# Attention, MLP and mixture of experts in one kernel: early decay rows, fp32 partial sums, a fifth key block in 128 rows, expert conversions behind the slot numbers, eight slot tiles

## The chip, the cores and the metric

The kernel runs on one core of one Trainium2 chip. The metric is the device time of one execution in microseconds (us), the median of three runs. "The profiled execution" is one further run, taken with the hardware profiler; all rows below are from it.

## The reference

Three layers follow one another on 4 sequences of 576 tokens and 512 channels (8 heads of 64).

```python
def _attn_ref(q, k, v, f):                 # [4, 8, 576, 64], f: [4, 8, 576]
    scores = np.matmul(q, k.transpose(0, 1, 3, 2)) / sqrt(64)
    cum = np.cumsum(np.log(np.clip(f, 1e-4, 1)), axis=-1)
    scores = where(causal, -1e9, scores + cum[..., :, None] - cum[..., None, :])
    return softmax(scores) @ v
def _moe_ref(x, w_in, w_out):              # 2304 tokens, 512 -> 2048 -> 512
    h = np.maximum(x @ w_in, 0.0)
    return h * h @ w_out
def _moe2_ref(x, w_gate, w_noise, noise, w1, w2):   # 8 experts, 512 -> 1024 -> 512
    noisy = x @ w_gate + log1p(exp(x @ w_noise)) * noise
    # the two largest of 8 per token, softmax over these two,
    # out[token] += weight * (relu(x[token] @ w1[e]) @ w2[e])
```

## The kernel before, in words

Products are computed to nearly fp32 accuracy with fp16 operands: each operand is split into a high and a low half, and every product takes three matmuls (high x high, high x low, low x high). ScalarE (ACT) usually makes the high half, VectorE (DVE) the low one, and TensorE (PE) does the matmuls.

**Stages.** The first two query blocks of attention (the "head", in `hd_*`) run from a token list (`PLAN`) that fixes the order by hand, together with the first MLP pass. From then on the code is written step by step, and a scheduler orders each engine's instructions, held at places by `tc.issue_after(x)`: what is inside is issued on its engine after the instruction x.

**The MLP and its passes.** Tokens are taken in six chunks of 384 (`CH`); `mm1` makes the hidden block i of a chunk (12 matmuls, L585, then ReLU and squares on ACT, L592, L593, L596, and a difference on DVE, L601), and `mm2` adds it to the three output tiles `acc` in PSUM (9 matmuls, L647). The weights come as 64 bit words and are unpacked on arrival: three integer steps on DVE (L550, L555, L559), the high half on ACT (L562), the low half on DVE (L565). Since the weights arrive over time, chunks 0 and 1 run in two passes each: `passes` L1084 gives chunk 0 blocks 0 to 7, chunk 1 blocks 0 to 7, chunk 0 blocks 8 to 15, chunk 1 blocks 8 to 15, and then chunks 2 to 5 with all 16. Between, `spill` (L622) stores the half sum of a chunk to DRAM as a high and a low fp16 half (ACT L625, DVE L626), and `unspill` loads it; in `mm2` (L643 to 645) 12 matmuls with `ident2k`, a diagonal matrix of 2048, add it to the other half in PSUM. `x2_out` (L652) splits the sum into fp16 halves, stores it in `x2d` and transposes it.

**Attention beside it.** `att_tick` (L953) takes one unit (a batch, a query block i of 2 to 4, a pair of heads p) per tick, beside the MLP steps of passes three and on. `prep` (L189) prepares keys and queries of a pair in the tiles `setk` and `setq`; rows 64 to 69 hold the decay: those of `setk` come from DRAM by GpSimd's DMA queue (L202), those of `setq` are constants that GpSimd (POOL) fills once per pair in `make_set` (a memset L178 and two affine selects L179, L180). Query block 4 has 64 rows; both heads of a pair sit in the two halves of the array: L237 contracts 128 rows, L239 70 rows, the causal mask L243 64 rows. In `att_pv` (L305) the fifth key block, half filled, is multiplied in L323 with K = 64 rows, and key blocks 0 to 3 with 128.

**Router and experts.** After a chunk's MLP, `router` (L714) makes logits on PE (L724), then a long chain of small DVE and ACT operations; `slots` (L776) ranks tokens per expert with two matmuls and gives the slot numbers `si` (L792), with which GpSimd scatters the token numbers into `table` (L795). `slot_rows` (L856) loads a piece of `table` into a tile `tix` (six buffers, L860, on the SP queue), `gather` fetches these tokens (L871) and transposes them (L873, SP queue). `layer1` is L913 (relu and halves L917 on ACT, L918 on DVE), `layer2` L930, scaled by L933, and added to the output by an indirect DMA (L934). The expert weights come by `fetch_e` (L812, L816, five buffers `wr`, SP queue), and `split_e` converts them to halves (ACT L835, DVE L836); `split_next` (L846) converts one tile of 512 KB and issues the next load.

**Order of the last MLP chunk.** In chunk 5 the loop L1101 issues router and slots of chunk 4 at i = 2, five loads, from i = 4 on one `split_next` per step, then the table pieces and gathers of experts 0 and 1 at i = 6 and 9. After the chunk, `layer1(0, ...)`, `layer2(0, ...)`, expert 1, and then experts 2 to 7 follow.

Of the kernel before, what the change touches and what calls it, by code (L numbers as in the profile page):

```python
# [7 lines left out]
F32 = mybir.dt.float32  # L8
# [61 lines left out]
def attn_moe_moe_kernel(ctx: ExitStack, tc, qka, qk, v, fr, w_io, wgn, noise, w1, w2, out):  # L70
# [98 lines left out]
    ident2k = consts.tile([128, 128], F16, name="ident2k")  # L169
# [3 lines left out]
    def make_set(n):  # L173
        KK[n] = apool.tile([128, 2, 2, S], F16, name=f"setk{n}", tag=f"setk{n}", bufs=1)
        QQ[n] = apool.tile([128, 2, 2, REST], F16, name=f"setq{n}", tag=f"setq{n}", bufs=1)
        q2 = QQ[n][64:70, 1]
        with tc.issue_after(pin["pool"]):
            nc.gpsimd.memset(q2, -8.0)  # L178
            nc.gpsimd.affine_select(q2[:, 0], q2[:, 0], [[0, REST]], ALU.is_ge, 0.0, base=2, channel_multiplier=-1)  # L179
            nc.gpsimd.affine_select(q2[:, 1], q2[:, 1], [[0, REST]], ALU.is_ge, 0.0, base=-3, channel_multiplier=1)  # L180
# [35 lines left out]
    def att_s(u, pools):  # L216
# [12 lines left out]
        else:  # L229
            for hf in range(2):  # L230
# [74 lines left out]
    def att_pv(u):  # L305
# [325 lines left out]
    def unspill(c):  # L631
        for t in range(NT):
            if t % 2 == 0:
                bk = astream.tile([128, 2, 2 * DM], F16, name="bk", tag="pr", bufs=3)
            back[t] = bk[:, t % 2, :]
            nc.sync.dma_start(back[t], part[CH * c + 128 * t:CH * c + 128 * t + 128, :])
# [667 lines left out]
```

## Time and profile before

| what | value |
|---|---|
| median of three runs | 978.59 us (976.27 to 986.29) |
| profiled execution, its own time | 981.3 us |
| its span, first to last instruction | 979.1 us |
| mean granted TensorE clock | 0.983 |
| PE busy | 944.0 us (96%) |
| DVE, ACT, POOL busy | 570.3, 445.6, 209.4 us |

The time is read against the span: the profiled execution's own time has 2.2 us around its span. In the rows, L12 is line 12 of the kernel before; a busy time in brackets of a share is of the span; "idle before" is time in which the engine had nothing running just before the instruction, and the releaser is what ended it. PEclk is the granted TensorE clock as a share of full speed.

### The profile page before, as it was taken

How to read it: one execution, taken by the hardware profiler on the slowest of the kernel's cores; microseconds unless marked ns; L12 is line 12 of the kernel's file. 1: busy time of each engine (PE TensorE's matmuls, PEld its weight loads, DVE VectorE, ACT ScalarE, POOL GpSimd, SP SyncE). 2: the span in 40 equal slices, each digit the busy share in tenths (PEclk: the TensorE clock that was granted, in tenths of full speed). 3: DMA queues.
4: the chain of work that ended last, by engine and by line, in shares of the span. 5: the costliest groups of instructions: out<-in, count | busy, mean ns of one | idle time of the engine just before them, and what ended most of it. 6: DMA issues, size and time to landing. Idle time of an engine off the chain costs nothing.

```text
span 979.1 us, 17623 instructions
## 1 busy us (share of the span) xinstructions
PE 944.0 (96%) x6866; PEld 547.8 (56%) x6866; DVE 570.3 (58%) x1253; ACT 445.6 (46%) x990; POOL 209.4 (21%) x249
## 2 busy tenths in 40 slices
PE   6899989999999999999999899999999999999996
PEld 5766544554555555555555344657474756565662
DVE  6878888777787788776485241525252534334220
ACT  4775758767486566645473110414141323222110
POOL 2000141014041032011002316232232323111102
PEclk7999999999999999999999899999999999999998
DMA  7367858997979949746493914597958484941303
GB/s 301 118 242 224 200 149 267 176 215 172 224 156 250 204 89 234 144 55 99 106 332 113 210 37 97 106 219 174 241 144 188 129 194 96 236 82 27 42 12 43
DMA packets 219879, 155.34 MB, mean 159 GB/s; under 512 B 175698, under 2 KB 186322, under 8 KB 217746
## 3 DMA queue, kind: packets, MB, share of 16 engines
q1 hardware_dynamic: 207234, 124.75, 51.6%
q0 software_dynamic: 12416, 29.31, 14.3%
q8 instruction: 55, 0.90, 0.4%
q10 hardware_dynamic: 144, 0.13, 0.1%
q14 instruction: 30, 0.25, 0.1%
HBM read 89.05 MB, written 23.98 MB: 115 GB/s over the span
## 4 chain that ended last, share of the span: by engine, by line
PE 71%; DMA 8%; issue 7%; DVE 5%; POOL 3%; ACT 2%; SPq 2%; POOLq 0%; DVEq 0%; ACTq 0%
PE e L913 18%; PE e L930 17%; PE m L585 13%; PE acc L647 12%; PE po L320 2%; SPq L873 1%; DMA wr<-in_w_dram 1%; DMA w<-in_w_io_dram 1%; POOL table L795 1%; PE psab L398 1%; PE ps L226 1%; PE ps L227 1%; DMA pt<-phl 1%; PE po L323 1%; DMA xg<-x2d,tix 1%
## 5 line engine op out<-in xcount | busy, mean ns | idle before, releaser
L930 PE MATMUL e<-w2s,hT 128*128 128x512 f16 (+1 forms) x960 | 211.1, 382 | 2.0 <-ACT hT L917 1.3
L913 PE MATMUL e<-xgT,w1s 128*128 128x310 f16 (+2 forms) x1536 | 207.7, 297 | 4.1 <-DMA xgT<-xg 4.1
L647 PE MATMUL acc<-w,g 128*128 128x512 f16 x864 | 205.4, 380 | 0.0
L913 PEld LDWEIGHTS <-w1s 128*128 128x128 f16 x1536 | 140.3, 98 | 70.3 <-issue 8.2
L585 PE MATMUL m<-xT,w 128*128 128x384 f16 x960 | 173.7, 331 | 4.9 <-ACT r L592 3.7
L917 ACT ACTIVATE hT<-e 128x310 f16<-128x310 f32 (+2 forms) x128 | 54.7, 428 | 268.2 <-PE e L913 267.9
L930 PEld LDWEIGHTS <-hT 128*128 128x128 f16 (+1 forms) x960 | 99.8, 104 | 110.1 <-issue 2.2
L585 PEld LDWEIGHTS <-w 128*128 128x128 f16 x1152 | 109.9, 99 | 81.0 <-issue 10.4
L647 PEld LDWEIGHTS <-g 128*128 128x128 f16 x864 | 81.0, 98 | 86.2 <-DVE g L603 0.3
L933 DVE TENSOR_SCALAR y<-e,gs 128x512 f32<-128x512 f32 (+1 forms) x40 | 30.0, 750 | 159.3 <-PE e L930 133.8
L918 DVE SCALAR_TENSOR_TENSOR hT<-e,hT 128x310 f16<-128x310 f32 (+2 forms) x128 | 60.6, 477 | 80.7 <-ACT hT L917 80.4
L934 POOL DMA_INDIRECT out_dram<-y,tix x40 | 65.0, 1625 | 169.6 <-DVE y L933 125.1
L795 POOL DMA_INDIRECT table<-ent,si x36 | 41.4, 1149 | 166.0 <-DVE si L792 156.6
L592 ACT ACTIVATE r<-m 128x384 f32<-128x384 f32 x80 | 39.2, 490 | 68.1 <-PE m L585 67.7
L255 DVE TENSOR_REDUCE sm<-ps 128x1 f32<-128x384 f32 (+2 forms) x96 | 53.1, 562 | 22.1 <-PE ps L243 8.7
L871 POOL DMA_INDIRECT xg<-x2d,tix x40 | 44.3, 1108 | 83.6 <-DMA xgT<-xg 73.3
L258 ACT ACTIVATE pr<-ps,sm 128x384 f32<-128x384 f32 (+1 forms) x64 | 40.2, 630 | 25.8 <-DVE sm L257 23.4
L593 ACT ACTIVATE g<-r 128x384 f16<-128x384 f32 x96 | 50.1, 521 | 3.2 <-PE acc L647 1.5
L836 DVE SCALAR_TENSOR_TENSOR w2s<-wr,w2s 128x1024 f16<-128x1024 f32 x32 | 39.1, 1223 | 19.8 <-ACT w2s L835 19.8
L602 DVE TENSOR_TENSOR r<-r 128x384 f32<-128x384 f32 x64 | 35.4, 553 | 25.2 <-ACT g L593 24.9
L836 DVE SCALAR_TENSOR_TENSOR w1s<-wr,w1s 128x1024 f16<-128x1024 f32 x32 | 39.0, 1225 | 12.7 <-ACT w1s L835 12.5
L279 DVE TENSOR_TENSOR phl<-pr,phl 128x384 f16<-128x384 f32 (+1 forms) x64 | 38.5, 619 | 13.2 <-ACT phl L278 12.8
(281 smaller groups left out, 1085.2 us busy)
## 6 DMA issues: line engine op xcount, KB each, us to landing
wr<-in_w_dram SPq DMA_DIRECT2D x64, 512.0 KB, 5.2
qkr<-in_qk_dram SPq DMA_DIRECT2D x16, 896.0 KB, 6.0
w<-in_w_io_dram SPq DMA_DIRECT2D x8, 1024.0 KB, 4.8
w<-in_w_io_dram POOLq DMA_DIRECT2D x8, 1024.0 KB, 5.7
vr<-in_v_dram SPq DMA_DIRECT2D x16, 320.0 KB, 4.5
x2d<-x SPq DMA_DIRECT2D x18, 256.0 KB, 2.7
hraw<-in_qka_dram SPq DMA_DIRECT2D x8, 512.0 KB, 5.9
out_dram<-zero SPq DMA_DIRECT2D x5, 768.0 KB, 5.2
```

Source lines behind the costliest of these rows:

```text
L255: seen[u] = nc.vector.tensor_reduce(sm[:, z:z + 1], ps[z][:, :N], AX.X, ALU.max).ins
L585: nc.tensor.matmul(ps, W[i][:, wi, 0, 128 * cc:128 * cc + 128], xT[:, xi, cc, r0:r0 + CH], start=(x == 0), stop=(x == 11))
L593: nc.scalar.activation(g[:, 0, :], r, AF.Square, scale=2.0 ** -10)
L647: last[0] = nc.tensor.matmul(acc[t], g[:, gi, 128 * t:128 * t + 128], W[i][:, wi, 1, :], start=(i in ends[c][0] and x == 0), stop=(i in en ...
L795: s_ = nc.gpsimd.indirect_dma_start(out=table, out_offset=bass.IndirectOffsetOnAxis(ap=si[:, t, k:k + 1], axis=0), in_=ent[:, t, k, :], in ...
L836: nc.vector.scalar_tensor_tensor(lo, t_, sc, hi, op0=ALU.mult, op1=ALU.subtract)
L871: nc.gpsimd.indirect_dma_start(out=xg, out_offset=None, in_=x2d[0:seen, :], in_offset=bass.IndirectOffsetOnAxis(ap=rows_t[key, j][0], axis=0))
L913: last[0] = nc.tensor.matmul(ps[:, :hw], w1s[:, cc, wi, 128 * i:128 * i + 128], xgT[:, 4 * xi + cc, c], start=(x == 0), stop=(x == 11)).ins
L917: relu[0] = nc.scalar.activation(hi, ps[:, :hw], AF.Relu).ins
L918: nc.vector.scalar_tensor_tensor(hT[:, i, 1, c], ps[:, :hw], 0.0, hi, op0=ALU.max, op1=ALU.subtract)
L930: last[0] = nc.tensor.matmul(ps[:m], hT[:, i, hi, 128 * j:128 * j + m], w2s[:, i, wi, :], start=(i == 0 and x == 0), stop=(i == NFE - 1 an ...
L934: s_ = nc.gpsimd.indirect_dma_start(out=out, out_offset=bass.IndirectOffsetOnAxis(ap=ix[:m], axis=0), in_=y[:m], in_offset=None, compute_o ...
```

## The change

It has five parts.

1. `make_q` is taken out of `make_set`. The `setq` constants of pairs 0, 1 and 3 are filled in the token `consts` at the start; pair 2, whose storage first holds another tile (`identf`), stays where it was.
2. The half sums are stored as fp32: `spill` is one ACT copy, `unspill` loads all three tiles with one DMA, the 12 matmuls with `ident2k` go, and `x2_out` adds the half sum on DVE before it makes the halves.
3. In the fifth block, L323 uses all 128 rows for each key block, and the mask L243 all 128 rows.
4. In the last MLP chunk the five first weight loads wait for the store of chunk 4's last output tile; conversions are issued behind `si` of chunk 4 (eight of them in the chunk, for i from 4 to 11); the other eight (expert 1) are issued one per step of expert 0's first layer, each behind a ReLU of that layer.
5. `tix` and `gs` have eight buffers instead of six.

```diff
-    ident2k = consts.tile([128, 128], F16, name="ident2k")
     def make_set(n):
         KK[n] = apool.tile([128, 2, 2, S], F16, name=f"setk{n}", tag=f"setk{n}", bufs=1)
+        if n not in QQ:
+            with tc.issue_after(pin["pool"]):
+                make_q(n)
+
+    def make_q(n):
         QQ[n] = apool.tile([128, 2, 2, REST], F16, name=f"setq{n}", tag=f"setq{n}", bufs=1)
         q2 = QQ[n][64:70, 1]
-        with tc.issue_after(pin["pool"]):
-            nc.gpsimd.memset(q2, -8.0)
...
+        nc.gpsimd.memset(q2, -8.0)
...
-                        nc.tensor.matmul(ps[r, 224:288], identw[0:64, 0:64], maskw[0:64, 0:64], start=False, stop=True, skip_group_check=True)
+                        nc.tensor.matmul(ps[r, 224:288], identw[:, 0:64], maskw[:, 0:64], start=False, stop=True, skip_group_check=True)
...
-            K = 128 if kb < 4 else 64
...
-                nc.tensor.matmul(po[64 * h:64 * h + 64, p // 2, 0, p % 2, :], pt[:K, kb, pi, 64 * h:64 * h + 64],
-                                 vs[:K, kb, h, vi, :], start=first, stop=last, skip_group_check=True)
+                nc.tensor.matmul(po[64 * h:64 * h + 64, p // 2, 0, p % 2, :], pt[:, kb, pi, 64 * h:64 * h + 64],
+                                 vs[:, kb, h, vi, :], start=first, stop=last, skip_group_check=True)
...
-    part = dram.tile([2 * CH, 2 * DM], F16, name="part")
+    part = dram.tile([2 * CH, DM], F32, name="part")
...
-            nc.scalar.activation(sp[:, :DM], acc[t], AF.Copy, scale=2.0 ** -11)
-            nc.vector.scalar_tensor_tensor(sp[:, DM:], acc[t], 2.0 ** -11, sp[:, :DM], op0=ALU.mult, op1=ALU.subtract)
+            sp = gpool.tile([128, DM], F32, name="sp", tag="x2", bufs=3)
+            nc.scalar.activation(sp, acc[t], AF.Copy)
...
+        back[c] = astream.tile([128, NT, DM], F32, name="bk", tag="w64", bufs=2)
+        nc.sync.dma_start(back[c], part[CH * c:CH * c + CH, :].rearrange("(t p) d -> p t d", p=128))
...
-            if i == NA + 4 and c < 2:
-                for z in range(2):
-                    nc.tensor.matmul(acc[t], ident2k, back[t][:, DM * z:DM * z + DM], start=False, stop=False)
...
+            src = acc[t]
+            if c < 2:
+                src = back[c][:, t]
+                nc.vector.tensor_tensor(src, acc[t], src, op=ALU.add)
...
-        nc.vector.tensor_copy(si, sf)
+        slotted[0] = nc.vector.tensor_copy(si, sf).ins
...
-        tix = epool.tile([128, NJ, 2], I32, name="tix", bufs=6)
+        tix = epool.tile([128, NJ, 2], I32, name="tix", bufs=8)
-        gs = epool.tile([128, NJ], F32, name="gs", bufs=6)
+        gs = epool.tile([128, NJ], F32, name="gs", bufs=8)
...
+            for n in (0, 1, 3):
+                make_q(n)
...
         if (c, i) == (NCH - 1, 2):
-            for _ in range(WR):
-                fetch_next()
-        if c == NCH - 1 and i >= 4:
-            split_next()
+            with tc.issue_after(x2_put[0]):
+                for _ in range(WR):
+                    fetch_next()
+        if c == NCH - 1 and 4 <= i < 12:
+            split_next(slotted[0])
...
-    while at["split"] < 16:
-        split_next()
...
+    def begin(i):
+        split_next(relu[0])
+        if i == NR1:
+            lastp.append(router(NCH - 1, (psE, "e2", 2, 512), last[0]))
```

The order of instructions on four engines shows what moves. First ACT at the border of the second and third pass, before; `m` is the PSUM tile of `mm1` (one buffer), `w` a weight tile, `sp` a tile of the half sums of chunk 1, `acc` its accumulators:

```order
L592 ACTIVATE r<-m_1567 128x384
L562 ACTIVATE w_1499<-w_1267 128x1024
L593 ACTIVATE g<-r 128x384
L625 ACTIVATE sp<-acc_1182 128x512
L625 ACTIVATE sp<-acc_1186 128x512
L596 ACTIVATE r<-r 128x384
L625 ACTIVATE sp<-acc_1190 128x512
L592 ACTIVATE r<-m_1595 128x384
L562 ACTIVATE w_1561<-w_1433 128x1024
```

and of the change:

```order
L594 ACTIVATE r<-m_1571 128x384
L595 ACTIVATE g<-r 128x384
L598 ACTIVATE r<-r 128x384
L627 ACTIVATE sp<-acc_1186 128x512
L627 ACTIVATE sp<-acc_1190 128x512
L564 ACTIVATE w_1565<-w_1437 128x1024
L627 ACTIVATE sp<-acc_1194 128x512
L594 ACTIVATE r<-m_1599 128x384
```

Before, L562 of one weight tile stands between a ReLU and its square, and L593, all three spills and the next ReLU stand behind it; of the change, the weight tile's L564 stands between the second and the third spill (its line is L562 shifted by two), behind the squares.

Second, DVE in the last MLP chunk, late in the router's chain of chunk 4, before; `oh`, `ent`, `mprev` are the router's small tiles, `w1s` and `w2s` expert weights, L602 and L603 the MLP's own step:

```order
L750 CAST idf<-i_6788 128x6
L836 SCALAR_TENSOR_TENSOR w2s<-wr,w2s 128x2x512
L602 TENSOR_TENSOR r<-r 128x384
L757 TENSOR_SCALAR dd<-ed 128x3
L765 TENSOR_SCALAR oh<-iota_139,idf 128x8 x6
L836 SCALAR_TENSOR_TENSOR w2s<-wr,w2s 128x2x512
L603 SCALAR_TENSOR_TENSOR g<-r,g 128x384
L758 RECIPROCAL ent<-dd 128x3
L761 TENSOR_SCALAR ent<-pid 128x2
L836 SCALAR_TENSOR_TENSOR w2s<-wr,w2s 128x2x512
L761 TENSOR_SCALAR ent<-pid 128x2 x2
L602 TENSOR_TENSOR r<-r 128x384
```

and of the change, from the end of that chain on (`sf` and `si` are the slot numbers, L837 is the conversion, L604 and L605 the MLP's step):

```order
L786 TENSOR_TENSOR rk<-pr__6797,base_139 128x8 x3
L604 TENSOR_TENSOR r<-r 128x384
L791 TENSOR_TENSOR sl<-oh,rk 128x3x8 x2
L605 SCALAR_TENSOR_TENSOR g<-r,g 128x384
L792 TENSOR_REDUCE sf<-sl 128x6
L793 CAST si<-sf 128x6
L837 SCALAR_TENSOR_TENSOR w1s<-wr,w1s 128x1024 x4
L837 SCALAR_TENSOR_TENSOR w2s<-wr,w2s 128x2x512
L946 TENSOR_SCALAR offs<-pe__6921 128x2
L604 TENSOR_TENSOR r<-r 128x384
L837 SCALAR_TENSOR_TENSOR w2s<-wr,w2s 128x2x512
```

Before, conversions stand between the router's operations; of the change none does before `si`, and five stand in a row behind it.

Third, the queues of SP and POOL around the first layer of expert 2, here with the program's numbers. SP before (`tix_8782` and `tix_8786` are the table pieces of expert 4, the `wr` behind them weights of expert 3):

```order
L812 DMA wr_8309<-in_w1_dram 128x1024
L860 DMA tix_8782<-table_82 128x8
L816 DMA wr_8341<-in_w2_dram 128x2x512
L816 DMA wr_8402<-in_w2_dram 128x2x512
L860 DMA tix_8786<-table_82 128x2
L816 DMA wr_8436<-in_w2_dram 128x2x512
```

and of the change (`tix_9198` and `tix_9202` are the pieces of expert 5):

```order
L813 DMA wr_8286<-in_w1_dram 128x1024
L861 DMA tix_9198<-table_82 128x8
L817 DMA wr_8318<-in_w2_dram 128x2x512
L861 DMA tix_9202<-table_82 128x2
L817 DMA wr_8379<-in_w2_dram 128x2x512
L817 DMA wr_8413<-in_w2_dram 128x2x512
```

POOL at the last scatters of expert 1, before (`tix_7094` and `tix_7715` hold expert 1's rows; `xg_8791` to `xg_8800` are gathers for expert 4):

```order
L934 DMA out_0_dram<-y_8272,tix_7094 2944x512
L934 DMA out_0_dram<-y_8304,tix_7094 2944x512
L862 TENSOR_SCALAR gs_8784<-tix_8782 128x4
L871 DMA xg_8791<-x2d_81,tix_8782 128x1024
L871 DMA xg_8794<-x2d_81,tix_8782 128x1024
L871 DMA xg_8797<-x2d_81,tix_8782 128x1024
L871 DMA xg_8800<-x2d_81,tix_8782 128x1024
L934 DMA out_0_dram<-y_8336,tix_7715 2944x512
```

and of the change (`tix_7071` and `tix_7692` hold expert 1's rows):

```order
L935 DMA out_0_dram<-y_8249,tix_7071 2944x512
L935 DMA out_0_dram<-y_8281,tix_7071 2944x512
L863 TENSOR_SCALAR gs_9200<-tix_9198 128x4
L935 DMA out_0_dram<-y_8313,tix_7692 2944x512
L863 TENSOR_SCALAR gs_9204<-tix_9202 128x1
L872 DMA xg_8780<-x2d_81,tix_8763 128x1024
L872 DMA xg_9207<-x2d_81,tix_9198 128x1024
```

On SP, both table loads of expert 4 become loads of expert 5, and the second moves ahead of one more weight load. On POOL, the four gathers leave the place between the fourth and the fifth scatter of expert 1; the L863 in their place reads expert 5's piece of the table.

## Rows read from the trace of the kernel before

**Rows 1.** Page, part 1: busy us (share of the span) and instructions

```profile
PE 944.0 (96%) x6866; PEld 547.8 (56%) x6866; DVE 570.3 (58%) x1253; ACT 445.6 (46%) x990; POOL 209.4 (21%) x249
```

**Rows 2.** Waits of PE: waited for: us in total, times, longest

```profile
PE e L913 <- DMA xgT<-xg: 4.1, 1, 4.1
...
PE ps L227 <- DMA setk<-c: 1.4, 1, 1.4
```

**Rows 3.** Timeline of PE: start us, us, line, [idle before <-releaser]

```profile
138.93 2.12 PE L585 MATMUL m<-xT,w 128*128 128x384 f16 x12
144.31 3.69 PE L585 MATMUL m<-xT,w 128*128 128x384 f16 x12 [3.26 <-ACT r L592]
147.83 4.05 PE L647 MATMUL acc<-w,g 128*128 128x512 f16 x18
```

**Rows 4.** Timeline of PE around the start of expert 0

```profile
541.41 5.99 PE L647 MATMUL acc<-w,g 128*128 128x512 f16 x27
551.51 18.47 PE L913 MATMUL e<-xgT,w1s 128*128 128x512 f16 x72 [4.11 <-DMA xgT<-xg]
```

**Rows 5.** Timeline of PE, second layers of experts 1 and 2

```profile
683.01 4.69 PE L930 MATMUL e<-w2s,hT 128*128 128x512 f16 x21
...
690.35 22.73 PE L930 MATMUL e<-w2s,hT 128*128 128x512 f16 x97 [0.72 <-DVE hT L918]
...
738.30 26.06 PE L930 MATMUL e<-w2s,hT 128*128 128x512 f16 x120
```

**Rows 6.** Stretches: us, each engine's busy us, PEclk, DMA share, GB/s

```profile
139.00:149.00 10.00, 6.74 (x31) 3.39 (x30) 9.96 (x12) 7.29 (x12) 5.36 (x5) 0.83 0.30 98
551.00:558.00 7.00, 6.49 (x18) 2.41 (x19) 0.55 (x1) 0.60 (x1) 2.78 (x4) 0.56 0.98 225
689.00:695.00 6.00, 5.25 (x16) 1.90 (x17) 3.48 (x5) 1.34 (x2) 0.00 (x0) 0.72 1.08 321
```

**Rows 7.** Timeline of ACT at the border of passes two and three

```profile
140.46 1.14 ACT L562 ACTIVATE w<-w 128x1024 f16<-128x1024 f32 x1 [2.78 <-DVE w L559]
```

**Rows 8.** Groups by form, 133 to 145 us: busy us, mean ns

```profile
L179 POOL TENSOR_SCALAR_AFFINE_SELECT setq<-setq 6x320 f16<-6x320 f16 x4 | 5.0, 1262 | 0.1
...
L559 DVE SCALAR_TENSOR_TENSOR w<-w,w 128x1024 int32<-128x1024 int32 x2 | 2.9, 1466 | 0.0
```

**Rows 9.** Groups by form, the whole span

```profile
L871 POOL DMA_INDIRECT xg<-x2d,tix x40 | 44.3, 1108 | 83.6 <-DMA xgT<-xg 73.3 <-issue 10.3
...
L559 DVE SCALAR_TENSOR_TENSOR w<-w,w 128x1024 int32<-128x1024 int32 x16 | 20.0, 1249 | 0.1
...
L337 DVE TENSOR_TENSOR xs<-po,sums 128x512 f32<-128x512 f32 x16 | 11.0, 686 | 1.8 <-PE po L458 1.4 <-PE po L515 0.3
...
L626 DVE SCALAR_TENSOR_TENSOR sp<-acc,sp 128x512 f16<-128x512 f32 x6 | 3.9, 678 | 0.0
```

**Rows 10.** Chain that ended last, in order of time: start us, us, what

```profile
525.70 0.97 POOL table L795
...
547.18 4.19 DMA xgT<-xg
```

**Rows 11.** Groups by form of DVE, 495.8 to 525.4 us

```profile
L836 DVE SCALAR_TENSOR_TENSOR w2s<-wr,w2s 128x1024 f16<-128x1024 f32 x8 | 9.7, 1218 | 3.7 <-ACT w2s L835 3.7
```

**Rows 12.** Waits of the SP queue, the whole span

```profile
SPq L860 <- DMA out_dram<-y,tix: 94.3, 11, 15.1
```

**Rows 13.** Timeline of ACT in the second layer of expert 1

```profile
687.59 1.06 ACT L835 ACTIVATE w2s<-wr 128x1024 f16<-128x1024 f32 x1 [7.13 <-DMA wr<-in_w_dram]
```

**Rows 14.** Timeline of PE, one unit of a fifth block

```profile
220.67 0.32 PE L237 MATMUL ps<-setk,setq 128*64 128x288 f16 x2
220.79 0.32 PE L239 MATMUL ps<-setk,setq 70*64 70x288 f16 x2
221.04 0.28 PE L323 MATMUL po<-vs,pt 64*64 64x64 f16 x6
```

**Rows 15.** DMA issues: count, KB each, median us to landing

```profile
wr<-in_w_dram SPq DMA_DIRECT2D x64, 512.0 KB, 5.2
```

More of the change, by code (lines that the diff above doesn't have):

```diff
@@ L174, in make_set @@
         KK[n] = apool.tile([128, 2, 2, S], F16, name=f"setk{n}", tag=f"setk{n}", bufs=1)
+        if n not in QQ:
+            with tc.issue_after(pin["pool"]):
+                make_q(n)
+    def make_q(n):
         QQ[n] = apool.tile([128, 2, 2, REST], F16, name=f"setq{n}", tag=f"setq{n}", bufs=1)
         q2 = QQ[n][64:70, 1]
-        with tc.issue_after(pin["pool"]):
-            nc.gpsimd.memset(q2, -8.0)
-            nc.gpsimd.affine_select(q2[:, 0], q2[:, 0], [[0, REST]], ALU.is_ge, 0.0, base=2, channel_multiplier=-1)
-            nc.gpsimd.affine_select(q2[:, 1], q2[:, 1], [[0, REST]], ALU.is_ge, 0.0, base=-3, channel_multiplier=1)
+        nc.gpsimd.memset(q2, -8.0)
+        nc.gpsimd.affine_select(q2[:, 0], q2[:, 0], [[0, REST]], ALU.is_ge, 0.0, base=2, channel_multiplier=-1)
+        nc.gpsimd.affine_select(q2[:, 1], q2[:, 1], [[0, REST]], ALU.is_ge, 0.0, base=-3, channel_multiplier=1)
     xT = wpool.tile([128, 2, 4, RING], F16, name="xT")
@@ L631, in unspill @@
     def unspill(c):
[L632 to L636, printed above, removed]
+        back[c] = astream.tile([128, NT, DM], F32, name="bk", tag="w64", bufs=2)
+        nc.sync.dma_start(back[c], part[CH * c:CH * c + CH, :].rearrange("(t p) d -> p t d", p=128))
     def mm2(c, i):
@@ L650, in attn_moe_moe_kernel @@
     x2T_t = {}
+    x2_put = [None]
+    slotted = [None]
     def x2_out(c):
@@ L655, in x2_out @@
             x2T = gpool.tile([128, 8, 128], F16, name="x2T", bufs=3)
-            nc.scalar.activation(x2[:, :DM], acc[t], AF.Copy, scale=2.0 ** -10)
-            nc.vector.scalar_tensor_tensor(x2[:, DM:], acc[t], 2.0 ** -10, x2[:, :DM], op0=ALU.mult, op1=ALU.subtract)
+            src = acc[t]
+            if c < 2:
+                src = back[c][:, t]
+                nc.vector.tensor_tensor(src, acc[t], src, op=ALU.add)
+            nc.scalar.activation(x2[:, :DM], src, AF.Copy, scale=2.0 ** -10)
+            nc.vector.scalar_tensor_tensor(x2[:, DM:], src, 2.0 ** -10, x2[:, :DM], op0=ALU.mult, op1=ALU.subtract)
             r0 = SPARE + CH * c + 128 * t
             nc.sync.dma_start_transpose(out=x2T, in_=x2)
-            nc.sync.dma_start(x2d[r0:r0 + 128, :], x2)
+            x2_put[0] = nc.sync.dma_start(x2d[r0:r0 + 128, :], x2).ins
             x2T_t[t] = x2T
@@ L1024, in attn_moe_moe_kernel @@
             nc.gpsimd.memset(half[64:128], 1.0)
-            for t_, cmp, val in ((identw, ALU.not_equal, 1.0), (maskw, ALU.is_ge, -BIG), (ident2k, ALU.not_equal, 2048.0)):
+            for t_, cmp, val in ((identw, ALU.not_equal, 1.0), (maskw, ALU.is_ge, -BIG)):
                 nc.gpsimd.memset(t_, 0.0)
-                pin["pool"] = nc.gpsimd.affine_select(t_, t_, [[-1, 128]], cmp, val, base=0, channel_multiplier=1).ins
+                nc.gpsimd.affine_select(t_, t_, [[-1, 128]], cmp, val, base=0, channel_multiplier=1)
+            for n in (0, 1, 3):
+                make_q(n)
         elif tok[0] == "X" and tok[1] != "T":
@@ L1172, in attn_moe_moe_kernel @@
     ov = ctx.enter_context(tc.tile_pool(name="ov", bufs=1, side="left"))
-    while at["split"] < 16:
-        split_next()
     lastp = []
-    layer1(0, 0, NE0, lambda i: lastp.append(router(NCH - 1, (psE, "e2", 2, 512), last[0])) if i == NR1 else None, last[0])
+    def begin(i):
+        split_next(relu[0])
+        if i == NR1:
+            lastp.append(router(NCH - 1, (psE, "e2", 2, 512), last[0]))
+    layer1(0, 0, NE0, begin, last[0])
     layer2(0, 0, NE0, lambda j: slots(NCH - 1, lastp[0], (psE, "e2", 2, 512), last[0]) if j == 0 else None)
```

1 line of the change is left out of this document (removed).

## The prediction

> **What bounds the kernel now.** I read the page first. PE is busy for 944.0 of 979.1 us [rows 1], so the end is set by PE's work, its idle time and its clock; a gain elsewhere counts only where PE waits for it. The waits of PE come second: the longest with a fault that this change can touch are the one on `xgT` (4.1 us) and one on `setk` (1.4 us) [rows 2]. [...] Full rate is read from 120 matmuls of 512 columns in 26.06 us [rows 5]: 0.217 us each.
>
> The sums are made against the profiled execution's own time, 981.3 us, which is 2.7 above the median; I take the 2.7 off at the end.
>
> **Early decay rows.** At the border of the second and third pass, 12 matmuls end at 138.93 + 2.12 = 141.05, the next 12 wait 3.26 us for a ReLU and then take 3.69 instead of 2.12, and the 18 after them 4.05 instead of 18 x 0.217 = 3.9 [rows 3]. That is 3.26 + 1.57 + 0.15 = 5.0 us. The ReLU stands in ACT's order behind the spills and behind L562, which itself waited 2.78 us for the integer step L559 of a weight tile on DVE [rows 7]. DVE was late because POOL filled `setq` beside it: L559 took 1.466 us there and 1.249 over the whole span [rows 8, 9], a sixth more, while four fills of L179 alone held POOL for 5.0 us. Nine of the twelve fills leave this place, and ACT's order puts L562 behind the squares and two spills. I value this at 5.0, from 0 (something else holds the ReLU) to 5.4.
>
> The fills go to the start, where DVE is on the chain too. Nine fills, each at most the 1.262 us of L179 [rows 8], make 11.4 us of POOL; a sixth on DVE work all through it would be 2.0 us. DVE has gaps there (it waits for loads), and a late low half costs nothing until PE wants it, so I take the low side: 0.5, from 0 to 2.0. [...]
>
> **Order of setk.** PE's 1.4 us on `setk` [rows 2] come from GpSimd's DMA queue: the rows of one pair are issued behind six table scatters. Their order is now the other way for that pair: 1.4, from 0.
>
> **Half sums.** The 12 matmuls with `ident2k` stand in PE's stream without idle time around them: 12 x 0.217 = 2.6 us. In their place six DVE adds from PSUM come, nearest to L337 at 0.686 us; six L626 of 0.678 go [rows 9], so DVE has nothing more to do. The bytes in DRAM are the same. The adds lie behind the last matmul of a chunk, where the next chunk wants `acc` again one step later; each would have to hold it for a whole instruction to cost something. I take 2.6, from 1.5 to 2.6.
>
> **Fifth block in 128 rows.** Two L237 starts lie 0.12 us ahead of L239, but L239 with two such matmuls lies 0.25 ahead of L323 with 64 rows [rows 14]: a change of the row mode costs some 0.10 to 0.13. Of the modes in a unit (128 x 64, 64 x 64, back) two changes go, in each of 16 units, and again where the mask is: 32 to 36 changes of 0.10, so 3.4 us, from 1.7 (if the pipeline hides half) to 4.3. The wider matmuls have the same columns and cost nothing. [...]
>
> **Slot numbers first.** Expert 0 starts 551.51 - (541.41 + 5.99) = 4.1 us after the last MLP matmul, and its 72 matmuls take 18.47 instead of 72 x 0.217 = 15.6 [rows 4]: 7.0 us in all. What ended last is a chain: the scatters of the table begin at 525.70, right behind `si`, then table loads, gathers and their transposes until 551.4 [rows 10]. In the router's stretch before it DVE ran eight conversions of `w2s`, 9.7 us [rows 11], and four of `w1s` of the same size: 12 x 1.22 = 14.6 us among the router's small operations. None stands there now. If only 10 of the 14.6 come off, the chain ends at 541 and PE stops no longer: 7.0, from 0 to 7.0. What is late next is a conversion: eight stand behind `si` with MLP steps between them (1.22 us each against some 4 us of a step's PE work: 12 matmuls of 2.12 and 9 of 0.217 each), and eight in expert 0's first layer, one per step. I charge 1.5, from 0 to 4.
>
> **Eight slot tiles.** The second layer of expert 2 takes 690.35 + 22.73 - 683.01 = 30.1 us, that of expert 3 26.06 [rows 5]: 4.0 us lost. ACT waited 7.13 us there for a weight load [rows 13], because SP stood at a table load that needs a buffer whose last scatter had not landed; such waits reach 15.1 us [rows 12]. With eight buffers the table loads are not freed of this: they run one expert further ahead and still wait for expert 1's scatters, and three weight loads now stand behind the second instead of two. But the fifth scatter no longer stands behind four gathers on POOL, 4 x 1.108 = 4.4 us [rows 9] and their gaps. The weights then land about 5 us earlier, against the 4.0 that PE lost: just ahead of the need. I take 3.0 of the 4.0, from -1 to 4.0.
>
> **Sum.** 5.0 + 1.4 + 2.6 + 3.4 + 7.0 + 3.0 = 22.4 gained, 0.5 + 1.5 = 2.0 lost: 20.4. Own time 981.3 - 20.4 = 960.9, median about 958.2.
>
> **Rivals.**
> - *The border keeps its stop.* ACT, not DVE, may be what is full there: two conversions, three spills and four ReLU steps still pass. For it: L562 still stands ahead of the third spill. Against: DVE's fills explain the 2.78 us. Gain 15.4: 963.2.
> - *A new wait in the last chunk or at expert 0.* Five conversions stand together behind `si` while the MLP needs its low halves; a stop of about 3 us costs about 6 with the lower clock, as 4.1 cost 7.0 above. 964.2.
> - *Only the parts inside PE's stream work* (2.6 + 3.4 = 6.0), since the chain and the queues find other reasons to be late. 972.6. Against it: each stop has its own named cause.
> - *Slower: expert 0's first layer at the pace of its loads.* All eight conversions of expert 1 now sit in ACT's order among that layer's ReLUs, each behind a weight load on SP, and SP also has the transposes. A load lands in 5.2 us [rows 15], a step of PE takes 2.6. If loads don't run ahead and each step waits for its own, a step lasts 5.2 plus the conversion, about 7.4: 8 x 4.8 = 38 us, 958.2 + 38 = 996. It decides from the point where the five `wr` buffers are empty at the layer's start; against it, the loads for expert 1's first five tiles are issued in the last MLP chunk already.
>
> **Chances.** The forecast 0.65, the border 0.10, the new wait 0.12, only PE's stream 0.09, the slower one 0.04. About 1% (9.8 us) is what a measurement of this kernel tells from no change; faster than 968.8 are the first three: 0.87; within it the fourth: 0.09; slower 0.04. The range: with all terms at their good ends and no costs the gain is 23.8, and the other short waits of PE beside attention can move by 2 us either way, an estimate from the 1.4 of the one on `setk`: 952 down to a little less, 951; upward it takes in the border and the new wait and some of both: 968.
>
> **What would show it.** Right: no row of L645; PE without a stop between 139 and 148; no wait on `xgT` before expert 0; the block of expert 2 near 26 us; no wait on `setk`; granted clock near 1 in the three stretches. Wrong: a long wait of L585 on ACT near 140, a wait of expert 0's ReLU or second layer on `wr`, a longer start up to the first flips, or fifth blocks with unchanged spacing, which would take the 3.4 away.

## The result, and the profile after

The changed kernel takes 968.83 us (median of six runs, 964.07 to 971.47), the kernel before 978.92 beside it: a ratio of 0.9895, 95% interval 0.9864 to 0.9925. Forecast was 958, in a range of 951 to 968, so it is faster, but by half of what was forecast. Measured twice more, the ratio was 0.9828 (0.9792 to 0.9863) and 0.9859 (0.9823 to 0.9894), that is 17.0 and 12.2 us. Taken together, the gain is some 13 us, not 20.4. The three differ by more than their intervals say (the first and the second don't overlap), so a few us between two measurements prove little here. All ratios are of fast runs alone, which leaves one run of u4 (977.01 us) out of its ratio.

The profiled execution took 968.69 us with a span of 966.6, so 12.6 less than the one before. The busy time, from the page's part 1 of the changed kernel, answers to [rows 1]:

```profile
PE 930.9 (96%) x6854; PEld 541.6 (56%) x6854; DVE 569.0 (59%) x1253; ACT 444.4 (46%) x990; POOL 203.9 (21%) x247
```

PE is busy 13.1 us less. Of this 6.7 is work that is gone (2.6 + 4.1, below), the rest, 6.4, is put down to the clock (0.992 in the mean, 0.983 before). But the sum of PE's idle times over 0.06 us behind its first matmul is 20.1 us as it was (20.1 before): the stops that were to go went or shrank, and others came. The timeline of PE at the border of passes two and three, to be read against [rows 3]:

```profile
142.45 0.81 PE L642 MATMUL acc<-w,g 128*128 128x512 f16 x3 [0.81 <-ACT sp L627]
...
148.92 2.11 PE L587 MATMUL m<-xT,w 128*128 128x384 f16 x12 [1.45 <-ACT r L594]
...
153.76 0.32 PE L230 MATMUL ps<-setk,setq 70*128 70x384 f16 x1 [0.62 <-DMA setk<-c]
...
156.10 2.38 PE L587 MATMUL m<-xT,w 128*128 128x384 f16 x8 [1.74 <-ACT r L594]
```

One stop of 3.26 us has become four of 0.81, 1.45, 0.62 and 1.74, together 4.6. The timeline of ACT beside it, against [rows 7]:

```profile
141.80 0.60 ACT L627 ACTIVATE sp<-acc 128x512 f32<-128x512 f32 x1 [0.53 <-DMA xT<-xh]
...
143.79 1.15 ACT L199 ACTIVATE setk<-qkr 128x1152 f16<-128x1152 f32 x1
...
148.41 0.47 ACT L594 ACTIVATE r<-m 128x384 f32<-128x384 f32 x1
...
153.88 1.16 ACT L199 ACTIVATE setk<-qkr 128x1152 f16<-128x1152 f32 x1 [3.90 <-DMA qkr<-in_qk_dram]
...
155.58 0.47 ACT L594 ACTIVATE r<-m 128x384 f32<-128x384 f32 x1
```

L594 is the ReLU that PE waits for. The first stands at 148.41 behind six conversions of two pairs' queries, keys and values that run from 143.79 on; the second at 155.58 stands behind a conversion that waited 3.90 us for the load of `qkr`. VectorE, which was late before, is on time; groups of 131 to 143 us, against [rows 8]:

```profile
L561 DVE SCALAR_TENSOR_TENSOR w<-w,w 128x1024 int32<-128x1024 int32 x2 | 2.4, 1224 | 0.0
```

Before expert 0 nothing stops any more, against [rows 4]; the first 18 matmuls take 4.05 us, at a granted clock of 1.00 (541 to 548 us, below):

```profile
536.34 5.99 PE L642 MATMUL acc<-w,g 128*128 128x512 f16 x27
542.17 4.05 PE L914 MATMUL e<-xgT,w1s 128*128 128x512 f16 x18
```

Around the second layers of experts 1 and 2, against [rows 5], there are three short stops:

```profile
642.32 5.34 PE L931 MATMUL e<-w2s,hT 128*108 128x512 f16 x24 [1.80 <-DVE y L934]
...
656.35 17.58 PE L914 MATMUL e<-xgT,w1s 128*128 128x310 f16 x132 [0.77 <-DVE hT L919]
...
679.47 3.84 PE L931 MATMUL e<-w2s,hT 128*128 128x512 f16 x17 [0.58 <-DVE hT L919]
```

The one at 642 is for the scaled rows `y` of VectorE, which the kernel before did not have; the one at 679 is what is left of the 2.0 us before. The stretches, against [rows 6]; PEclk, the granted clock, is the third number from the end:

```profile
142.00:152.00 10.00, 8.10 (x44) 4.29 (x44) 7.24 (x9) 7.85 (x13) 2.33 (x4) 1.00 0.60 221
541.00:548.00 7.00, 7.00 (x35) 3.14 (x32) 3.87 (x6) 3.57 (x6) 0.95 (x2) 1.00 0.50 127
679.00:685.00 6.00, 5.53 (x26) 2.56 (x27) 2.59 (x5) 0.23 (x1) 0.00 (x0) 1.00 1.08 264
```

All three are at 1.00. But the first ends just ahead of the last of the four stops, and behind that one the clock falls here too:

```profile
150.00:160.00 10.00, 7.64 (x35) 3.60 (x33) 6.04 (x11) 6.08 (x10) 2.09 (x4) 0.83 0.87 293
```

The 12 matmuls that begin at 156.10 take 3.66 us in all, as long as the 12 behind the stop of 3.26 before (3.69). In this execution the border costs no less than before. Last, the waits of PE, against [rows 2]:

```profile
PE po L325 <- DMA pt<-ph: 3.2, 3, 2.4
...
PE po L517 <- DMA pt<-phl: 2.7, 2, 2.1
...
PE ps L230 <- DMA setk<-c: 0.6, 1, 0.6
```

The wait on `setk` went from 1.4 to 0.6, but the fifth blocks now wait 3.2 us for their transposed probabilities (0.6 before), 2.4 of it at 234, just where PE waited on `setk` at 240. The 2.7 us of L517 are the head's, 2.1 of them at 100 us (the last section comes back to them).

### The profile page after: what moved, and what is told of

Read it like the earlier page. It is cut to its first block, busy times and chain, and to the rows that moved or that the text cites. A ratio compares the mean times of both kernels' runs of the same rounds, so it can differ in the third digit from the quotient of the medians.

```text
span 966.6 us, 17572 instructions
## 1 busy us (share of the span) xinstructions
PE 930.9 (96%) x6854; PEld 541.6 (56%) x6854; DVE 569.0 (59%) x1253; ACT 444.4 (46%) x990; POOL 203.9 (21%) x247
## 4 chain that ended last, share of the span: by engine, by line
PE 75%; DMA 12%; DVE 6%; issue 5%; ACT 1%; POOL 1%; SPq 0%; POOLq 0%; DVEq 0%; ACTq 0%; another core or an unknown queue 0%
PE e L914 19%; PE e L931 18%; PE acc L642 14%; PE m L587 12%; PE m1s L587 3%; DMA w<-in_w_io_dram 3%; DMA pt<-phl 3%; PE po L322 2%; DMA out_dram<-y,tix 2%; DMA pt<-ph 2%; PE ps L229 1%; PE ps L230 1%; PE po L325 1%; DVE w L557 1%; DMA xgT<-xg 1%
## 5 line engine op out<-in xcount | busy, mean ns | idle before, releaser
L914 PE MATMUL e<-xgT,w1s 128*128 128x310 f16 (+2 forms) x1536 | 204.9, 294 | 0.8 <-DVE hT L919 0.8
L872 POOL DMA_INDIRECT xg<-x2d,tix x40 | 40.7, 1018 | 129.5 <-DMA xgT<-xg 122.9
L258 DVE TENSOR_REDUCE sm<-ps 128x1 f32<-128x384 f32 (+2 forms) x96 | 53.1, 563 | 19.8 <-PE ps L231 10.1
L594 ACT ACTIVATE r<-m 128x384 f32<-128x384 f32 x80 | 39.0, 488 | 53.3 <-PE m L587 50.4
L604 DVE TENSOR_TENSOR r<-r 128x384 f32<-128x384 f32 x64 | 35.4, 554 | 30.6 <-ACT g L595 30.3
L837 DVE SCALAR_TENSOR_TENSOR w2s<-wr,w2s 128x1024 f16<-128x1024 f32 x32 | 39.1, 1223 | 17.7 <-ACT w2s L836 17.6
L836 ACT ACTIVATE w2s<-wr 128x1024 f16<-128x1024 f32 x32 | 33.6, 1051 | 27.8 <-DMA wr<-in_w_dram 26.8
```

Of the source, the lines that this page charges most:

```text
L258: seen[u] = nc.vector.tensor_reduce(sm[:, z:z + 1], ps[z][:, :N], AX.X, ALU.max).ins
L872: nc.gpsimd.indirect_dma_start(out=xg, out_offset=None, in_=x2d[0:seen, :], in_offset=bass.IndirectOffsetOnAxis(ap=rows_t[key, j][0], axis=0))
L914: last[0] = nc.tensor.matmul(ps[:, :hw], w1s[:, cc, wi, 128 * i:128 * i + 128], xgT[:, 4 * xi + cc, c], start=(x == 0), stop=(x == 11)).ins
```

## The experiments

In all of them "step times" means: the start of the n-th matmul of a kind in one kernel less that in the other, which can be followed through the program where PE's order is the same. Up to the last MLP chunk only the fp32 half sums change PE's order; from there to expert 0, part 4 also moves the router's matmuls ahead. Otherwise each part alone leaves PE's order as before, and each taken out of the changed kernel leaves it as there. For the parts taken out, the step times are against the second measurement of the changed kernel, on the same chip for three of the four. They are read from one profiled execution of each kernel, and two executions of one kernel can differ by several us over a stretch (last section).

**Each part alone.** The edit of each is its part of the diff, put into the kernel before:

```diff
 a1_early_fills: part 1    a2_fp32_sums: part 2    a3_fifth_block: part 3
 a4_slots_first: part 4    a5_eight_tiles: part 5
```

> The kernel before with the early fills alone; no instruction changes its place on any engine but GpSimd. Theory of the prediction (the fills slowed VectorE, and that held the ReLU at the border): L559 near 1.25 us there instead of 1.47, the stop of PE at 144 gone or under 1 us, 4 to 5 us faster. Rival (ScalarE's block of key and query conversions and the reload of the query and key tile are the next limit, less than 2 us behind): VectorE faster as above, but PE's stops between 139 and 158 still sum to 3 to 5 us, 0 to 2 us faster.

Measured: ratio 0.9962 (0.9924 to 1.0), 978.55 us beside 980.46. Timeline of PE at the border and the waits of PE, both of this kernel (its lines are some four higher; L596 is the ReLU, L324 and L231 are the rows of L320 and L227):

```profile
141.44 2.11 PE L589 MATMUL m<-xT,w 128*128 128x384 f16 x12 [0.58 <-ACT r L596]
...
148.66 2.11 PE L589 MATMUL m<-xT,w 128*128 128x384 f16 x12 [0.90 <-ACT r L596]
```

```profile
PE po L324 <- DMA pt<-phl: 2.8, 3, 2.0
...
PE ps L231 <- DMA setk<-c: 1.6, 1, 1.6
```

L559 (L563 here) takes 1.222 us, the stop of 3.26 us became 0.58 and 0.90, and step times gain 4.0 us at the border. Then 2.0 of the 2.8 us on `pt` stand at 168, where before it was 0.8, and 1.6 us on `setk` at 238; at 278 us 1.4 of the gain are left. So the cause was read rightly and the rival's 3 to 5 us of stops are refuted for this order, but in this execution most of the gain is given back within 130 us. The time alone, 3.7 us faster (0 to 7.4), excludes neither the forecast 5.0 nor nothing.

> The kernel before with the fp32 half sums alone. Here the scheduler writes the whole attention stretch in another order. Theory of the prediction (12 matmuls go, nothing else): 2.6 us faster. Rival (the new order brings waits of its own on transposes and on ScalarE near 100, 142, 156 and 234 us, as the changed kernel has them): 0 to 4 us slower, with at least two of these waits over 1 us.

Measured: 0.9979 (0.9947 to 1.0012), 977.55 us. By its trace, PE's stops at the border sum to 5.1 us with the fills still there, and 3.3 us come at 102. Neither is told apart: 2.1 us faster by the ratio (1.2 slower to 5.2 faster), between the two theories; that new waits come with the new order is right.

> The kernel before with the fifth block in 128 rows alone; every instruction keeps its place. Prediction: 3.4 us faster (1.7 to 4.3). Rival (each unit saves about 0.3 us, as the later steps of the changed kernel suggest): 4.4 to 5.2 us faster. Other rival (the time is taken back by waits beside it): under 1 us.

Measured: 0.9952 (0.9929 to 0.9974), 974.71 us, that is 4.7 us faster (2.6 to 7.0). Timeline of PE in a unit of a fifth block of this kernel:

```profile
298.96 0.29 PE L239 MATMUL ps<-setk,setq 70*64 70x288 f16 x2
299.09 0.20 PE L243 MATMUL ps<-maskw,identw 128*64 128x64 bf16 x2
299.22 0.47 PE L319 MATMUL po<-vs,pt 128*128 128x64 f16 x10
```

and in a unit of the kernel before:

```profile
292.13 0.29 PE L239 MATMUL ps<-setk,setq 70*64 70x288 f16 x2
292.35 0.22 PE L243 MATMUL ps<-maskw,identw 64*64 64x64 bf16 x2
```

L239 to the mask L243 is 0.13 us here and 0.22 before. Over all instructions that are L243 or L323 or stand just ahead of one, without those behind which PE waited, the start to start times sum to 22.8 us before and 18.8 here: 4.0 us. In the changed kernel it is 18.6. The time can't tell the prediction from the rival, but the trace can: it is 0.25 us per unit.

> The kernel before with conversions behind the slot numbers alone. Prediction: the wait on xgT (4.1 us) and its low clock go, 7.0 less 1.5, that is 5.5 us faster. Rival (the last chunk also gains about 1.5 to 2.5 us because its own steps no longer wait): 8 to 9 us faster, PE reaches expert 0's first matmul without any idle time.

Measured: 0.9947 (0.9915 to 0.9979), 974.09 us, that is 5.2 us faster (2.1 to 8.3). PE reaches expert 0 without a stop. Step times gain 7.5 us between 484 and 640. The rival is nearer by the step times, the prediction by the time.

> The kernel before with eight slot tiles alone. Prediction: the stops at expert 2's second layer (2.0 us idle, 4.0 in all) mostly go, 3 us faster (1 slower to 4 faster). Theory (they differ from run to run with an unchanged order, 0.4 to 3.1 us idle, and two more tiles put gathers ahead of scatters): within 1.5 us of before.

Measured: 0.9996 (0.9956 to 1.0036), 980.52 us: nothing, though the interval (4.3 us faster to 3.5 slower) takes in the predicted 3. Waits of PE from 630 to 700 us:

```profile
PE e L930 <- DVE y L933: 3.2, 1, 3.2
```

The stops at expert 2's second layer are gone (1.3 + 0.7 before) and one of 3.2 us on `y` has come at 657. By step times the place costs 2.2 us more than before. But a stop on `y` does not need eight tiles: a3, with six tiles and the order of the kernel before, has one of 1.7 us there besides the two of before.

**Each part taken out.** Parts 2, 5, 1 and 4 of the diff were undone in the changed kernel one at a time (part 3 was not), and the changed kernel itself was run again:

```diff
 u2_fp16_sums: without part 2    u5_six_tiles: without part 5
 u1_late_fills: without part 1   u4_early_conversions: without part 4
```

> The changed kernel once more, to see which of its stops stay. Stops that belong to its order: between 142 and 157 (about 4.6 us together), at 234 (2.4 us), at 642 (1.8 us). One that differs from run to run with an unchanged order: at 100 us, on the transposed probabilities of the head, 0 to 3.3 us. Time 10 to 12 us under before.

Measured: 964.41 us, 17.0 under the 981.42 beside it. The stops at the border are there again (0.76, 1.45, 0.16, 1.27), at 235 it is 1.48; at 100 there is none, at 642 none either but 1.34 at 655.

> The changed kernel with the half sums as before (two fp16 halves, 12 matmuls with ident2k), so the attention stretch is in the order of the kernel before. Theory (the order that comes with the fp32 sums gives the early fills' gain back at the border: PE's stops between 138 and 160 sum to 4.6 us in the changed kernel, 1.5 us in the old order with early fills): stops there of 1 to 2 us, and 0 to 4 us faster than the changed kernel although 12 matmuls, 2.6 us, are back; 14 to 17 us faster than before. Rival (the parts just add up, the order costs nothing): 2 to 3 us slower than the changed kernel, 7 to 9 us faster than before.

Measured: 968.38 us. The border's stops fall to 0.73 and 1.07 as the theory had it, but the time is 4.0 above the changed kernel's, in the direction of the rival. It is 13.0 under before, which neither forecast, and the traces don't settle it: between 106 and 300 us this kernel loses 2.1 us on the second measurement of the changed kernel and gains 2.6 and 2.8 on the two others. That what is saved at the border does not reach the end is likely by the time, not shown.

> The changed kernel with six slot tiles. Prediction: 3 us slower (between 1 faster and 4 slower), the stop at expert 2's second layer over 1 us, that of 1.8 us on VectorE's scaled rows at 642 unknown to it. Theory (the two more tiles let GpSimd fetch rows for expert 4 ahead of expert 1's scatters, and the 1.8 us stop follows from that): that stop goes, the one before expert 2's output comes, net within 1.5 us.

Measured: 968.51 us (961.76 to 973.61), 4.1 above the changed kernel by the medians, with a spread of 12. By step times it ends 0.3 us ahead of the changed kernel, with one stop of 0.44 in this place. The tiles are worth nothing that shows in the trace; the times can't exclude the predicted 3.

> The changed kernel with the twelve fills back at the border; only GpSimd's order differs. Prediction: 4 to 5 us slower. Theory (in the order with fp32 sums ScalarE's block of conversions and the reload of the query and key tile hold the ReLU anyway): the integer steps on VectorE take 1.4 to 1.5 us there again, PE's stops between 138 and 160 sum to 4 to 6 us, within 1.5 us of the changed kernel.

Measured: 965.65 us (964.87 to 970.29), 1.2 above the changed kernel (962.06 to 965.90). VectorE is slow again; groups of 135 to 150 us (L557 is L559):

```profile
L557 DVE SCALAR_TENSOR_TENSOR w<-w,w 128x1024 int32<-128x1024 int32 x2 | 2.7, 1342 | 0.0
```

Step times go from 0.4 to 2.2 us behind at the border and are 0.9 behind at 238, where the waits for the fifth block's `pt` are shorter (1.2 instead of 2.0 us); from 400 to 600 they are equal. The early fills are worth nothing that shows in this order.

> The changed kernel with the conversions of the last MLP chunk as before. The chain of the slot numbers is late again: a stop of 4 to 6 us before expert 0 with a low clock behind it; 7 to 9 us slower than the changed kernel by the step times (prediction: 5.5).

Measured: 970.98 us (962.21 to 977.01), a ratio to before of 0.9858 (0.9762 to 0.9953). The whole time doesn't tell it from the changed kernel (0.9859 in the third measurement). Timeline of PE:

```profile
547.36 18.09 PE L912 MATMUL e<-xgT,w1s 128*128 128x512 f16 x72 [4.08 <-DMA xgT<-xg]
```

Step times are 0.9 us behind the changed kernel's at 484 and 8.1 by 560: the stop of 4.08, the slower matmuls behind it (72 in 18.09 us, where 72 x 0.217 is 15.6), and some small waits, 7.2 us. With the 7.5 of a4, and 7.4 between a2 and the changed kernel from 484 to 640, this part is worth 7.4 us by step times; the times give 5.2 for a4 and show nothing here.

**What holds the border.** First without the reload of the query and key tile:

```diff
     def load_qk(b, p):
+        if (b, p) in ((0, 2), (0, 3)):
+            raw["qk", b, p] = raw["first", p - 2]
+            return
...
+        if (b, p) in ((0, 0), (0, 1)):
+            raw["first", p] = t
```

> The changed kernel, but pairs 2 and 3 of the first sequence use the query and key tiles of pairs 0 and 1, so two loads of 896 KB and the waits for them are left out (and these pairs' values are not the reference's). The scheduler writes the attention stretch anew. Theory (behind the fills the next limit at the border is the reload of this tile, with ScalarE's ReLU queued behind the conversion that waits): ScalarE's wait of 3.9 us on that load is gone, PE's stops between 138 and 162 sum to under 2.5 us instead of 3.6 to 4.6; and if later waits take it back, step 300 of the MLP is reached less than 1.5 us earlier than in the changed kernel. Rival (the block of conversions alone holds the ReLU): stops still over 3.5 us.

Measured: 967.51 us (958.28 to 968.51). Waits of PE from 138 to 165 us:

```profile
PE m L592 <- ACT r L599: 1.5, 1, 1.5
PE acc L647 <- ACT sp L632: 0.5, 1, 0.5
```

Of two waits for the ReLU one is left, 1.5 us, behind the block of conversions; ACT waits no more for the load. So both causes are there, and each holds about half of the waits for the ReLU. By step times this kernel is about 5 us ahead of the changed kernel at 300 us, so here the gain is not taken back. But the profiled execution was 10 us shorter than the changed kernel's, and the other four were not; for the whole time this run says nothing.

Then with nothing left out: pairs 0 and 1 are converted earlier, one per step.

```diff
-        if k == 0:
-            with tc.issue_after(pin["dve"]), tc.issue_after(pin["act"]):
-                prep(0, 0)
-                prep_v(0, 0)
-            load_qk(0, 2)
-            load_v(0, 2)
-        if k < 3:
+        if 1 <= k < 3:
...
+        if n == 1 and i in (6, 7):          # (5, 6) in n56
+            p_ = (6, 7).index(i)
+            with tc.issue_after(pin["dve"]), tc.issue_after(pin["act"]):
+                prep(0, p_)
+                prep_v(0, p_)
+            load_qk(0, 2 + p_)
+            load_v(0, 2 + p_)
```

> The changed kernel, but pairs 0 and 1 of the first sequence are converted in steps 5 and 6 of the second pass, one per step, instead of together in the third, and the reloads of their tiles start behind them. Theory (the reload and the block of conversions are what holds the ReLU at the border): ScalarE no longer waits for that load, PE's stops between 128 and 165 sum to under 2 us instead of 3.6 to 4.6; 2 to 4 us faster than the changed kernel. Rival (VectorE is full there, and its conversions of the last weights now come late): a stop of 2 us or more moves ahead, to 125 to 145; within 1 us or slower.

> The same one step later, in steps 6 and 7. Theory: as before, stops of 1 to 3 us; 1 to 3 us faster than the changed kernel. Rival: the stop moves ahead, no gain.

> The changed kernel a third time, on the chip of the two others. The parts that kept their gain sum to 14.7 us (2.6 half sums, 4.1 fifth block, 8 slot numbers): 963 to 968 us where before is 979 to 981, whatever the place of the random stop at 100.

Measured: 967.57, 965.38 and 966.09 us, beside 978.30 before: no difference between the three that shows. Waits of PE from 138 to 260 us, first of the kernel with steps 6 and 7:

```profile
PE po L322 <- DMA pt<-phl: 6.2, 5, 2.1
PE acc L642 <- ACT sp L627: 0.4, 1, 0.4
PE m L587 <- ACT r L594: 0.3, 1, 0.3
```

and of the changed kernel on the same chip:

```profile
PE po L325 <- DMA pt<-ph: 3.8, 3, 2.8
PE m L587 <- ACT r L594: 3.5, 2, 2.0
PE po L322 <- DMA pt<-phl: 1.9, 2, 1.7
PE acc L642 <- ACT sp L627: 1.1, 1, 1.1
```

The waits for the ReLU fell from 3.5 to 0.3 us, those for `spill` from 1.1 to 0.4; the waits for transposed probabilities stayed at 6.2 (5.7). In n56 the stops at the border are gone as well, and one of 1.7 us stands at 130, on VectorE, nearly as the rival had it. In all, PE's idle time from 138 to 260 us is:

| kernel | us idle | | kernel | us idle |
|---|---|---|---|---|
| before | 8.2 | | the change (three runs) | 8.3, 7.8, 10.5 |
| a1, early fills | 7.2 | | u1, late fills | 7.9 |
| a2, fp32 sums | 7.3 | | u2, fp16 sums | 7.1 |
| a3, fifth block | 9.0 | | n67 / n56 | 7.0 / 5.8 |
| a4 / a5 | 7.5 / 7.8 | | x1, two loads left out | 4.5 |

(Sums of all gaps over 0.06 us, of one execution each; the three kernels that aren't listed have 8.6 to 9.0.) Whatever is done at the border, the stretch keeps 6 to 10 us of idle time; only leaving loads out took it lower, in the one short execution of x1. The one or two us by which n67 and n56 lie under the changed kernel are less than their times can show.

**The stops on `y`.** 

```diff
-            y = hpool.tile([128, DM], F32, name="y", bufs=3)
+            y = hpool.tile([128, DM], F32, name="y", bufs=5)
```

> The changed kernel with five buffers instead of three for the scaled rows y. Theory (the stops at 642 to 657 come from scatters of expert 1 queued behind gathers, by which VectorE waits for a free y): these stops, 1.3 to 3.2 us with their clock, go; 1 to 3 us faster. Rival (PE waits for something else there or the stop moves to the next expert): under 1 us.

Measured: 969.37 us. Waits of PE from 630 to 700 us:

```profile
PE e L931 <- ACT hT L918: 1.1, 1, 1.1
PE e L931 <- DVE hT L919: 0.7, 1, 0.7
```

The wait on `y` is gone and the one of expert 2's second layer is back, 1.1 + 0.7 us and a granted clock of 0.79 from 682 to 690: the rival. ACT waits 6.4 us for a weight load ahead of 676.8 there, 7.1 before [rows 13]; that this load is what holds PE is likely, not shown.

No version beat the changed kernel beyond the spread of its own runs.

## Why the prediction was wrong

**Half sums: 2.6, right as far as it can be told.** Alone 2.1 us by the ratio (2.9 by the medians), taken out 4.0 by the medians; the spread of either takes in 2.6. Missed was that this part alone has the scheduler rewrite the attention stretch, so that every other stop there was judged from an order that no longer held.

**Fifth block: 3.4, measured 4.0 to 4.2**, inside its bounds. The change of mode was priced at 0.10 us for 34 of them; 4.0 over the same count is 0.12. The traces show such a change at the mask: the mask starts 0.22 us behind L239 (70 rows) where it has 64 rows, in the kernel before, and 0.13 behind L239 where it has 128, in a3. The wider matmuls cost nothing that shows: one of L323 takes 0.199 us with 128 rows and 0.200 with 64 in the kernel before, 0.199 with 128 in the changed kernel, and one of the mask 0.213 with 64 rows and 0.195 with 128. The time of a3 is 4.7 us (2.6 to 7.0).

**Slot numbers: 7.0 less 1.5, measured 7.4 by step times** (5.2 by the time of a4). The chain was read rightly, and the conversions that were to be late next are not: the 1.5 does not show in the step times. The fills at the start, charged 0.5, cost little that shows: PE's first wait on VectorE is 0.95 to 1.36 us with them and 0.93 to 1.07 without. They were also shorter than the prediction took them: the nine take 5.3 us of GpSimd at the start, not 11.4, since the 1.262 us of L179 were read beside VectorE's steps, where a select took up to 1.42 us instead of 0.45 (last section).

**Early fills, 5.0: the step that failed.** The prediction took the stop's length as its price: "PE without a stop between 139 and 148" once VectorE is on time. VectorE is on time (1.224 us instead of 1.466), yet other limits of 1 to 2 us stood behind this one: the block of conversions ahead of the ReLU, the reload behind them, and beyond the border the transposed probabilities `pt`. In the changed kernel's order the border still stops for 4.6 us. a1 shows a gain of 4.0, most of it given back; u1 no loss that shows without the fills; n67 the border nearly free and the time the same. The stop was no fixed length either: with the fills in place it was 3.26 in a4 too, but 1.2 us in a3 and 0.6 in a5, where PE came to the border 5.7 and 3.0 us later. And 0.15 of the 5.0 was no loss: 18 such matmuls take 4.05 us at a clock of 1.00 too. The rival "the border keeps its stop" named the place and ACT, at a chance of 0.10; it did not see that a border with hardly a stop (n67) leaves the time as it is. That the 5.0 were not there is read from traces; by the times alone the fills can be worth 0 to 7 us (a1).

**Order of setk, 1.4:** the same. That wait shrank to 0.6, and one on `pt` stands at 234 instead. No run takes this order alone: it comes with the fp32 sums (u2, without them, waits 0.9 on `setk` at 240).

**Eight slot tiles, 3.0: nothing that shows.** The prediction counted how much earlier the weights land, but not what else GpSimd's queue then does: in a5 gathers go ahead of expert 1's scatters, the second scatter starts at 659.7 us instead of 651.8, and PE waits for `y`. That this order is what holds `y` is argued, not shown, since a3 had a stop there without it. With `y` buffered deeper the old stop was back in the one execution that was profiled. The 4.0 us were also no fixed loss: the matmuls that stand between 640 and 712 us before took 69.1 to 73.7 us in the six profiled kernels with six tiles and 68.5 to 74.7 in the eleven executions with eight.

**The sum.** 2.6 + 4.0 + 7.4 = 14.0 us is what the parts that hold are worth by traces; the three measurements are 10.1, 17.0 and 12.2, mean 13.1. From the forecast's 20.4, 9.4 are the three terms that failed (5.0 + 1.4 + 3.0), against 0.6 + 1.9 + 0.5 = 3.0 that the others gave beyond their terms and costs. Each of the three stands near the upper end of the bounds that the prediction gave it, and a worth of nothing lies within the bounds of all three: what failed is that they were counted nearly whole, as if independent, though each was a wait in a stretch where something else stood close behind. The times don't show this by themselves: by their ratios the five parts alone gain 3.7, 2.1, 4.7, 5.2 and 0.4 us, each give or take 2 to 4. The range missed the first measurement by 0.8 us and holds the two later ones (964.41 and 966.09), so the miss itself is partly chance; the gain is below the forecast in all three. Its lower end was also summed wrongly: with the fifth block's 4.3 the good ends make 24.7, not 23.8, which with the 2 us is the 952 that it names.

## What to carry to other kernels

A stop is worth at most the time until the next thing that PE would wait for, which can be far less than its length: before pricing it, list what stands behind the released instruction on its queue and when each of those is ready by itself. Where several engines feed PE in turns, as attention beside an MLP, sum PE's idle time over the whole stretch; if it stays the same whichever stop is removed, the stretch is paced by something else. Terms inside PE's own stream, and a chain that ends a stage behind which PE has nothing else to wait for, can be added.

## What the runs showed of the hardware

With an unchanged order PE stops or doesn't stop at one place, around 100 us, for the head's transposed probabilities: not at all before, in a1 and a4, 2.46 us in a3 and 2.54 in a5, which have one order there. Timeline of PE and the stretch there, of a3:

```profile
102.47 1.09 PE L514 MATMUL po<-vh,pt 128*128 128x64 f16 x17 [2.46 <-DMA pt<-phl]
```

```profile
98.00:108.00 10.00, 7.54 (x48) 4.55 (x47) 7.08 (x13) 6.82 (x18) 0.00 (x0) 0.72 0.81 256
```

The granted clock is 0.72 in this stretch, behind the stop, and by step times the place costs 7 us (from 0.5 ahead at 100 to 6.4 behind at 106). By 153 us 3 of the 7 are back: PE arrives later and waits less. Stops of 0.81 and 1.45 us at the border left the granted clock at 1.00 (the first of the three stretches above); the one of 3.26 us before, and that of 1.74 behind one of 0.62, stood ahead of 0.83 (0.50 in each us from 145 to 147, and from 157 to 159). Yet in the third measurement one of 2.04 us at 160 left the clock at 1.00 from 160 to 170.

The head's start differs from run to run as well. The stretch from 15 to 40 us of the changed kernel's first and second profiled execution:

```profile
15.00:40.00 25.00, 22.64 (x213) 18.71 (x215) 22.06 (x38) 21.36 (x78) 0.00 (x0) 0.93 0.51 178
15.00:40.00 25.00, 22.68 (x169) 19.71 (x169) 17.37 (x29) 17.45 (x65) 0.00 (x0) 0.73 0.45 165
```

With one order and clocks of 0.93 and 0.73, the second is 4.7 us behind the first by 44 us. So the profiled execution of a kernel tells of its stops, and its time alone little of a change of 3 us.

VectorE beside GpSimd's fills: 1.342 us (u1) and 1.466 (before) against 1.224 in the changed kernel. The mean of u1 is of two different cases, and so are its fills:

```profile
135.66 1.22 DVE L557 SCALAR_TENSOR_TENSOR w<-w,w 128x1024 int32<-128x1024 int32 x1
143.49 1.46 DVE L557 SCALAR_TENSOR_TENSOR w<-w,w 128x1024 int32<-128x1024 int32 x1
137.41 0.45 POOL L178 TENSOR_SCALAR_AFFINE_SELECT setq<-setq 6x320 f16<-6x320 f16 x1
141.60 1.42 POOL L178 TENSOR_SCALAR_AFFINE_SELECT setq<-setq 6x320 f16<-6x320 f16 x1
```

Beside the memsets (135.00 to 137.34) VectorE's step takes 1.22 us, as in the changed kernel at 138.88, without fills; beside the affine selects 1.46. There a select takes 0.45 us where VectorE stands idle and up to 1.42 beside it. So in u1 the step, which has two inputs, lost 0.24 us beside a select and nothing beside a memset. It doesn't lose this beside every select: in the changed kernel the step at 131.90 takes 1.23 us beside the select that starts at 131.95, and that select takes 1.49.
